# Scan and mixture of adapters on one core: stores of four chunks in 8 KB rows, other buffer counts, and orders as lists of names

## The chip, the core and the metric

The kernel runs on one core of one Trainium2 chip. Its engines are TensorE (PE in the profile), VectorE (DVE), ScalarE (ACT), GpSimd (POOL) and SyncE (SP), which here only issues DMAs. The metric is the device time of one execution in microseconds; the kernel before has a median of 202.84 us over 3 runs (202.61 to 203.44).

## What is computed

A linear recurrence over 6400 steps for 8 sequences of 128 channels, and then, on its 51200 output rows x, a mixture of adapters: of 8 experts of rank 16 the two with the highest logits are taken, weighted by a softmax over the two, and their outputs are added to x.

```python
for t in range(S):                       # a, b: [8, 6400, 128]
    h = a[:, t] * h + b[:, t]
    out[:, t] = h
x = out.reshape(51200, 128)
logits = x @ w_gate                      # [51200, 8]
# w: softmax over the two largest logits of each row, zero for the others
# out[row] = x[row] + sum over e of w[row, e] * ((x[row] @ A[e]) @ B[e])
```

With 8 x 16 = 128 the adapters of all experts are one 128x128 matrix A, whose product z is multiplied by the weights of the experts before the second matrix B. All inputs and the output are float32; 52.4 MB are read and 26.2 MB are written.

## The kernel before

The rows are cut into 100 chunks of 512 (names end in the chunk's number); a chunk is four blocks of 128 rows. What happens to a chunk falls into a front and a back.

**Front** (`load`, line 692; `front`, line 748). SP loads a and b of two chunks at a time, 512 KB each, into one of `NL` = 6 places of `a_tm` and `b_tm` (line 707). A partition takes eight rows in succession, 4 KB; the first four chunks are loaded singly, in 2 KB rows. The transposes `A`, `B` and `P` on PE (line 728) bring channels to the partitions in `pA` and `pB`, two places of PSUM each: `P93`, for example, transposes b of chunk 93 and a of chunk 94. ACT copies `pA` to `a_st` (`ae`, line 746), and DVE scans (`sc`, line 784) into `xT`, f16, which has `NX` = 24 places of one chunk.

**Logits and weights** (`zlogits`, line 795; `gating`, line 816). A unit is four or six blocks. PE multiplies each block of `xT` by A and the gate (`Z`, line 804), ACT copies the result to one of `NZ` = 120 places of `zl` (`ze`, line 810). For a group of one to four units DVE and POOL find the two largest logits, and ACT takes a sigmoid; the steps are `g1` to `g8`.

**Back** (`back_part`, line 899). POOL or DVE multiplies z by the weights (`mu`, `md`, lines 913 and 917), PE transposes the product (`T`, line 926), ACT or DVE copies it to `zwT` (`te`, lines 932 and 935), PE adds x and the product with B in `pO` (`D`, lines 940 and 941), and ACT or DVE copies the sum to `outt` (`oe`, `od`, lines 955 and 952), which has `NO` = 72 places of one block.

**Store** (`store`, line 976). SP stores two chunks at a time, 512 KB (line 986), the last four singly. A partition holds four rows in succession of each chunk, so a row of a store is 2 KB. `xblock` (line 665) picks the columns of `xT` that make a block: with four rows to a partition every fourth column belongs to one block, a step of 8 bytes.

```python
def xblock(b):
    return xcols(b // J).rearrange("d (p j) -> d j p", j=J)[:, b % J, :]
...
dst = out[r0 : r0 + m * C, :].rearrange("(h p j) d -> p h j d", p=128, j=J)
view = outt[:, q : q + m * J, :].rearrange("p (h j) d -> p h j d", j=J)
```

**Order.** Every step is an `Op` with the ops that it depends on. `schedule` (line 330) goes through the ops by a rank: a base by the chunk, and a number of `NUDGE` (line 30). With `WINDOW` at 0 the order on each engine is that of the ranks. Which engine takes a step is in `GATE_DVE`, `TE_ACT`, `MU_DVE` and `OE_DVE`. `waits` (line 400) gives each op the semaphores that it waits for. Each engine, and SP's queue of DMAs, works strictly in its order: what stands behind a waiting op waits too. A load waits until the transposes of the pair six places earlier are done, a scan until `D` of the chunk 24 earlier is done, a copy to `outt` until the store that held its places has landed.

Of the kernel before, what the change touches and what calls it, by code (L numbers as in the profile page):

```python
# [10 lines left out]
PERIOD = 6  # L11
FREE = {"pe": 0.0, "act": 0.105, "dve": 0.082, "pool": 0.044, "sp": 0.0}
SEEN = {"pe": 0.06, "act": 0.04, "dve": 0.055, "pool": 0.08, "sp": 0.0}
SELF = {"pe": 0.0, "act": 0.035, "dve": 0.035, "pool": 0.078, "sp": 0.0}
PE_WAIT = 0.08
PE_FREE = 0.1
SP_MARGIN = 2.0
LAND_MARGIN = 1.0
Q_RATE = {3: 4.2e-3, 5: 2.1e-3, 7: 2.1e-3}
SCAN_SELF = 0.13  # L20
ISSUE = {"sp": 0.52, "act": 0.45}
LOAD_RATE = 387e3
STORE_RATE = 413e3
DMA_START = 0.3
DMA_SEEN = 1.15
DMA_DEPTH = 9
FIRST_ISSUE = 0.7
FIRST_WORK = 0.73
TABLES = 1.32
NUDGE = {  # L30
# [182 lines left out]
}  # L213
WINDOW = {'pe': 0.0, 'act': 0.0, 'dve': 0.0, 'pool': 0.0, 'sp': 0.0}
START = (-999, "", 0)
FIRST = -9999
EARLY = -400
LEAD = [1, 2]
# [886 lines left out]
```

## Time and profile before

| | |
|---|---|
| time, median of 3 runs | 202.84 us |
| span of the profiled execution, first to last instruction | 200.9 us |
| bytes moved by DMA, mean rate | 79.26 MB, 395 GB/s |
| landing of a load of 512 KB, from its issue (median) | 13.3 us for a, 13.5 us for b |
| landing of a store of 512 KB (median) | 13.4 us |
| mean granted clock of TensorE | 0.997 |

The profiled execution is one run, and its span stands beside the median of the runs: the difference, 1.9 us, lies outside of the first and last instruction. In the profile a line such as L986 is a line of the kernel; `out<-in` names what an instruction writes and reads; SPq is SP's queue of DMAs; PEld are the weight loads of PE, which overlap its matmuls. The busy time of PE holds the pipeline's latency of each matmul, so starts that follow each other say more of PE than durations.

### The profile page before, as it was taken

The numbers are of one execution on the slowest core, as the hardware profiler recorded it, in microseconds if no ns is written. First come the engines' busy times: TensorE is split into PE (matmuls) and PEld (weight loads), VectorE is DVE, ScalarE is ACT, GpSimd is POOL, SyncE is SP. The second block draws the span as 40 slices with busy tenths as digits, with TensorE's granted clock in tenths as the row PEclk, the third lists the DMA queues.
The fourth block names the chain that finished last, engine by engine and source line by source line (L and its number), as shares of the span: only waits on it lengthen the run. The fifth ranks groups of instructions, "written<-read, shape, count | busy, mean of one in ns | idle before, by whom it ended". The sixth has DMA issues, their size and how long they took to land.

```text
span 200.9 us, 7611 instructions
## 1 busy us (share of the span) xinstructions
PE 177.7 (88%) x3192; PEld 155.9 (78%) x3192; DVE 176.2 (88%) x283; ACT 175.8 (88%) x327; POOL 136.9 (68%) x176
## 2 busy tenths in 40 slices
PE   6888978999899969999988999899999997898970
PEld 6766867888688858888878888787888886787860
DVE  1699999999999968999897999798899998999971
ACT  2589998999779969999997999899999998899970
POOL 1331559498989887797987797868876466767420
PEclk9999999999999999999999999999999999999998
DMA  6999999999999999999999999999999999999985
GB/s 216 378 412 408 411 405 401 411 406 404 414 409 400 412 416 409 401 417 407 409 413 409 410 409 412 413 410 411 417 408 410 414 410 409 406 381 387 357 338 215
DMA packets 29065, 79.26 MB, mean 395 GB/s; under 512 B 2664, under 2 KB 2920, under 8 KB 29032
## 3 DMA queue, kind: packets, MB, share of 16 engines
q1 hardware_dynamic: 28456, 78.39, 99.0%
q8 instruction: 25, 0.41, 0.8%
q10 hardware_dynamic: 576, 0.40, 0.7%
q14 instruction: 8, 0.07, 0.1%
HBM read 52.56 MB, written 26.21 MB: 392 GB/s over the span
## 4 chain that ended last, share of the span: by engine, by line
DMA 33%; PE 27%; DVE 16%; ACT 15%; SPq 5%; issue 2%; DVEq 0%; ACTq 0%
DMA a_tm<-in_a_dram 26%; DVE xT L784 9%; DMA out_dram<-outt 7%; ACT zl L810 5%; PE pZ L804 5%; SPq L707 5%; PE pB L728 5%; PE pA L728 5%; ACT outt L955 4%; PE pO L940 4%; PE pO L926 4%; ACT a_st L746 4%; PE pO L941 3%; DVE zwT L935 2%; ACT zwT L932 2%
## 5 line engine op out<-in xcount | busy, mean ns | idle before, releaser
L784 DVE TENSOR_TENSOR_SCAN xT<-a_st,xT,pB 128x512 f16<-128x512 f32 x96 | 120.4, 1254 | 7.1 <-PE pA L728 4.3
L913 POOL TENSOR_TENSOR zw<-zl,g 128x512 f16<-128x512 f32 x88 | 92.7, 1067 | 27.9 <-DVE g L880 19.6
L728 PE MATMUL pB<-ident_f,b_tm 64*128 64x64 f32 (+1 forms) x784 | 69.3, 229 | 6.8 <-DMA a_tm<-in_a_dram 6.7
L728 PE MATMUL pA<-ident_f,a_tm 64*128 64x64 f32 (+1 forms) x784 | 69.8, 230 | 0.5 <-DMA b_tm<-in_b_dram 0.3
L746 ACT COPY a_st<-pA 128x512 f32<-128x512 f32 x100 | 63.3, 638 | 4.1 <-PE pA L728 3.3
L728 PEld LDWEIGHTS pB<-ident_f,b_tm 64*128 64x128 f32 (+1 forms) x784 | 56.4, 139 | 11.8 <-DMA a_tm<-in_a_dram 8.3
L810 ACT COPY zl<-pZ 128x816 f32<-128x816 f32 (+1 forms) x69 | 59.7, 865 | 2.0 <-PE pZ L804 1.7
L728 PEld LDWEIGHTS pA<-ident_f,a_tm 64*128 64x128 f32 (+1 forms) x784 | 56.8, 139 | 5.6 <-issue 0.4
L955 ACT COPY outt<-pO 128x512 f32<-128x512 f32 x88 | 55.9, 640 | 3.9 <-PE pO L941 3.0
L940 PE MATMUL pO<-ident_h,xT 128*128 128x128 f16 x368 | 51.6, 222 | 1.3 <-ACT zwT L932 1.0
L941 PE MATMUL pO<-cst_h,zwT 128*128 128x128 f16 x368 | 50.5, 219 | 0.0
L940 PEld LDWEIGHTS pO<-ident_h,xT 128*128 128x128 f16 x368 | 40.2, 113 | 4.3 <-ACT zwT L932 1.4
L804 PE MATMUL pZ<-cst_h,xT 128*128 128x136 f16 x400 | 35.9, 225 | 4.9 <-DVE xT L784 2.0
L941 PEld LDWEIGHTS pO<-cst_h,zwT 128*128 128x128 f16 x368 | 36.8, 100 | 0.0
L926 PE MATMUL pO<-ident_h,zw 128*128 128x128 f16 x368 | 35.2, 220 | 1.4 <-ACT outt L955 1.1
L804 PEld LDWEIGHTS pZ<-cst_h,xT 128*128 128x128 f16 x400 | 26.3, 114 | 9.1 <-DVE xT L784 4.3
L926 PEld LDWEIGHTS pO<-ident_h,zw 128*128 128x128 f16 x368 | 22.9, 97 | 4.7 <-ACT outt L955 1.3
L935 DVE COPY zwT<-pO 128x512 f16<-128x512 f16 x57 | 22.9, 407 | 4.0 <-PE pO L926 3.7
L932 ACT COPY zwT<-pO 128x512 f16<-128x512 f16 x35 | 21.9, 630 | 4.7 <-PE pO L926 4.3
L850 POOL TENSOR_TENSOR L<-k,m 128x192 f32<-128x192 f32 (+2 forms) x16 | 8.4, 524 | 6.2 <-DVE m L848 6.1
L872 POOL TENSOR_TENSOR k<-k,L 128x192 f32<-128x192 f32 (+1 forms) x17 | 9.4, 556 | 4.3 <-DVE L L868 3.0
L846 POOL TENSOR_TENSOR L<-L,k 128x192 f32<-128x192 f32 (+1 forms) x15 | 8.6, 576 | 5.4 <-DVE L L843 4.7
(58 smaller groups left out, 112.2 us busy)
## 6 DMA issues: line engine op xcount, KB each, us to landing
a_tm<-in_a_dram SPq DMA_DIRECT2D x48, 512.0 KB, 13.3
b_tm<-in_b_dram SPq DMA_DIRECT2D x48, 512.0 KB, 13.5
out_dram<-outt SPq DMA_DIRECT2D x47, 512.0 KB, 13.4
a_tm<-in_a_dram SPq DMA_DIRECT2D x4, 256.0 KB, 4.3
out_dram<-outt SPq DMA_DIRECT2D x4, 256.0 KB, 3.6
b_tm<-in_b_dram SPq DMA_DIRECT2D x3, 256.0 KB, 5.1
out_dram<-outt SPq DMA_DIRECT2D x1, 496.0 KB
b_tm<-in_b_dram ACTq DMA_DIRECT2D x1, 256.0 KB, 3.4
```

Source lines behind the costliest of these rows:

```text
L728: last = eng["pe"].transpose(*args)
L746: lambda: eng["act"].copy(a_st[c % NA][:, :], pA[:, c % 2, :]), fr(c, "ae"))
L784: last = eng["dve"].tensor_tensor_scan(out=x[:, s0:s1], data0=a_st[c % NA][:, s0:s1], data1=pB[:, c % 2, s0:s1], initial=init, op0=ALU.mul ...
L804: last = eng["pe"].matmul(pZ[:, k // (n // 2), o : o + W], xblock(b0 + k), Awg_h)
L810: return eng["act"].copy(zl[:, zb : zb + n, :].rearrange("p (h k) w -> p h (k w)", h=2), pZ[:, :, 0 : n // 2 * W])
L913: lambda: eng["pool"].tensor_tensor(out=wv, in0=zv, in1=gv, op=ALU.mult), ba(gi, c, "mu"))
L926: last = eng["pe"].transpose(ptile[:, k * 128 : k * 128 + 128], zz[:, k, :], ident_h[:, :])
L932: lambda: eng["act"].copy(zt, ptile[:, 0 : n * 128]), ba(gi, c, "ta"))
L935: lambda: eng["dve"].tensor_copy(zt, ptile[:, 0 : n * 128]), ba(gi, c, "te"))
L940: eng["pe"].matmul(dst, xblock(b0 + k), ident_h[:, :], start=True, stop=False)
L941: last = eng["pe"].matmul(dst, zt[:, k * 128 : k * 128 + 128], B_h, start=False, stop=True)
L955: lambda: eng["act"].copy(ov, bv), ba(gi, c, "oe"))
```

## The change

Stores take four chunks (1 MB) but for the first two (two chunks each) and the last four (single ones, as before). Over the chunks of one store a partition holds all rows in succession: 16 rows or 8 KB for four chunks, 4 KB for two. So the columns of `xT` that make a block are now every sixteenth of four chunks, a step of 32 bytes. `xT` is one tile, and the logits of a unit wait for the scan of the last chunk of its store; a place of `xT` is free when `D` of all four chunks of the store that held it are done. The fronts run on to the end of the store's chunks before the logits.

`NX` goes from 24 to 32, `NO` from 72 to 80, `NZ` from 120 to 96. Ahead of `P6` to `P13` PE runs four transposes of the identity each (`fi7` to `fi14`, into `pA`), which wait for the copy that frees the place. The planner with its ranks is gone: the order of each engine and of SP's queue is a list of names, and the engine of a step follows from the list in which it stands. DVE has 68 copies to `zwT` (60 before), 3 to `outt` (7) and 9 products with the weights (12); the other 32, 97 and 91 are ACT's, ACT's and POOL's; of the gating steps that either DVE or POOL can take, DVE has 28 (20 before).

The diff, cut to its core:

```diff
-TAIL_UNITS = [4, 4, 4, 4]
-HEAD_UNITS = [4, 4, 4]
-FILL = {}
-NX = 24
-NZ = 120
-NO = 72
-STORE_TAIL = [1, 1, 1, 1]
+UNITS = [4] * 3 + [6] * 62 + [4] * 4
+GROUPS = [1, 2] + [4] * 15 + [2, 1, 1, 1, 1]
+STORES = [2, 2] + [4] * 23 + [1] * 4
+FILL = {k: 4 for k in range(7, 15)}
+NX = 32
+NZ = 96
+NO = 80
+ORDER = {
+    "pe": (
...
+    "sp": (
+        "la1 la0 lb1 la2 la3 lb3 lb2 la4 lb4 la6 lb6 la8 lb8 la10 lb10 la12 lb12 la14 lb14 la16 lb16 la18 lb18 la20 "
+        "lb20 lb24 la22 lb22 la24 la30 la26 lb26 la28 st0 lb32 lb28 lb30 la36 la32 st4 la34 lb34 lb36 lb38 st2 la38 "
+        "lb40 la40 st8 la42 st12 lb42 la50 la44 lb44 la46 lb46 la48 lb48 st16 lb50 la54 la52 lb52 st20 lb54 la56 lb56 "
...
+        "lb76 la76 st36 lb78 la78 la80 la82 lb80 st40 lb82 lb84 la84 st44 st48 la86 lb86 la88 lb88 la90 lb90 st52 "
+        "la92 lb92 lb94 la94 la96 st56 lb96 la98 st60 st64 lb98 st68 st72 st76 st80 st84 st88 st92 st97 st96 st98 "
+        "st99 "
+    ),
+}
...
+        self.order = {e: [named[name] for name in ORDER[e].split()] for e in self.ENGINES}
...
-            return xT[c % NX][:, :]
+            o = c % NX * C
+            return xT[:, o : o + C]
 
         def xblock(b):
-            return xcols(b // J).rearrange("d (p j) -> d j p", j=J)[:, b % J, :]
+            s0, n = tile_of[b // J]
+            o = s0 % NX * C
+            return xT[:, o : o + n * C].rearrange("d (p j) -> d j p", p=128)[:, b - s0 * J, :]
...
+        def filler(c):
+            def f(e):
+                for _ in range(FILL[c]):
+                    last = e.transpose(pA[:, c % 2, 0:128], ident_f[:, :], ident_f[:, :])
+                return last
+
+            if c in FILL:
+                o_fi[c] = P.add("pe", f"fi{c}", FILL[c], get(o_ae, c - 2) + [o_id], f)
...
         def zlogits(u):
             b0, n = units[u]
-            c1 = (b0 + n - 1) // J
+            c1 = sum(tile_of[(b0 + n - 1) // J]) - 1
...
-            xlast[ch % NX] = o_D[c]
+            s0, m = tile_of[c]
+            for k in range(s0, s0 + m):
+                if xlast.get(k % NX, (None, []))[0] != s0:
+                    xlast[k % NX] = (s0, [])
+                xlast[k % NX][1].append(o_D[c])
...
-            dst = out[r0 : r0 + m * C, :].rearrange("(h p j) d -> p h j d", p=128, j=J)
-            view = outt[:, q : q + m * J, :].rearrange("p (h j) d -> p h j d", j=J)
+            dst = out[c * C : (c + m) * C, :].rearrange("(p j) d -> p j d", p=128)
+            view = outt[:, q : q + m * J, :]
```

In SP's list `la` and `lb` are loads of a and b (of a pair from chunk 4 on), and `st` is a store, each with its first chunk. The end of the old list, in the same names, is `la92 lb92 st58 la94 lb94 la96 st60 lb96 la98 st62 lb98 st64 st66` and then the stores that are left.

More of the change, by code (lines that the diff above doesn't have):

```diff
@@ L853, in maxes @@
[L853 to L862 removed]
+                return P.add("dve" if kind == 8 else "pool dve", f"g{kind}_{gi}", nb, deps, f)
@@ L937, in delta, with tr @@
-            def delta():
-                for k in range(n):
+            def tr(e):
+                for k in range(J):
+                    last = e.transpose(ptile[:, k * 128 : k * 128 + 128], zz[:, k, :], ident_h[:, :])
+                return last
+            o_T[c] = P.add("pe", f"T{c}", J, [o_mu[c], o_ih] + free + (o_wu if c < 2 else []), tr)
+            o_te[c] = P.add("dve act", f"te{c}", J, [o_T[c]] + get(o_D, c - NW),
+                            lambda e: copy(e, zt, ptile[:, 0:C]))
@@ L956, in back_part @@
-            for k in range(n):
+                    e.matmul(dst, xblock(b0 + k), ident_h[:, :], start=True, stop=False)
+                    last = e.matmul(dst, zt[:, k * 128 : k * 128 + 128], B_h, start=False, stop=True)
+                return last
+            o_D[c] = P.add("pe", f"D{c}", J, [o_te[c]], delta)
+            s0, m = tile_of[c]
[3 more added lines that the diff above has]
+                xlast[k % NX][1].append(o_D[c])
@@ L1012, in load_next, with fronts @@
-        def load_next(c):
-            if c not in o_la:
-                load(c, 1 if c < HEAD else HC)
-        nf, nb = 0, 0
+        def fronts(c):
+            s0, n = tile_of[c]
+            return s0 + n
+        nf, nb, ns = 0, 0, 0
         for gi, (u0, n) in enumerate(groups):
@@ L1032, in bass_associative_scan_2x2__then__mixture_of_adapters_kernel @@
                 nb += 1
+                if sum(stores[ns]) == nb:
+                    store(*stores[ns])
+                    ns += 1
         P.schedule()
-        waits = P.waits(s_eng, s_dma)
+        waits = P.waits()
         def run(name, handle):
```

607 lines of the change are left out of this document (171 added, 436 removed), and 235 rows, old and new, of tables (NUDGE, ORDER).

## The prediction

> **What bounds the kernel now.** First the page: the busy shares, the slices of the DMA engines, and the queue that SP feeds.
>
> ```profile
> span 200.9 us, 7611 instructions
> PE 177.7 (88%) x3192; PEld 155.9 (78%) x3192; DVE 176.2 (88%) x283; ACT 175.8 (88%) x327; POOL 136.9 (68%) x176
> DMA  6999999999999999999999999999999999999985
> GB/s 216 378 412 408 411 405 401 411 406 404 414 409 400 412 416 409 401 417 407 409 413 409 410 409 412 413 410 411 417 408 410 414 410 409 406 381 387 357 338 215
> ...
> q1 hardware_dynamic: 28456, 78.39, 99.0%
> ...
> HBM read 52.56 MB, written 26.21 MB: 392 GB/s over the span
> ```
>
> No engine is full, and each of the four has 23 us or more idle. The 16 DMA engines have no idle slice before the last five: from 5 us to 175 us they move about 410 GB/s. Next, the DMA view of three stretches: 12 to 24 us (only loads, in 4 KB rows: the first store is issued at 24.97 us), 60 to 160 us (two loads to a store), and 178.5 to 184.5 us, behind the last load, which SP issues at 162.58 us and which lands some 14 us later. There only stores run, in 2 KB rows. Columns of the q1 lines: packets, MB, share of the 16 engines.
>
> ```profile
> q1 hardware_dynamic: 1346, 4.88, 102.0%
> ...
> q1 hardware_dynamic: 14522, 40.77, 102.5%
> ...
> q1 hardware_dynamic: 1207, 2.32, 101.6%
> ...
> 24.97 0.40 SPq L986 DMA_DIRECT2D out_dram<-outt  x1
> ...
> 162.58 1.77 SPq L707 DMA_DIRECT2D b_tm<-in_b_dram  x1
> ...
> DMA to landing us min/median/max: 4.1/13.5/15.7
> ```
>
> That is 4.88/12 = 407 GB/s for loads, 40.77/100 = 408 for the mix and 2.32/6 = 387 for stores alone, with the engines full each time. So up to the last load the kernel is bound by the DMA queue. It is not bound tightly, as the waits show (first for the whole run, then for 160 to 180 us; total, times, longest):
>
> ```profile
> PE pB L728 <- DMA a_tm<-in_a_dram: 6.7, 10, 2.0
> ...
> PE pB L728 <- DMA a_tm<-in_a_dram: 1.5, 3, 1.1
> ```
>
> PE stands 6.7 us before loads that haven't landed. A faster queue can give back about that much before the order of the engines' own work is the limit. Last, the tail: scans of chunks 93 and 99 and the last copy to outt on DVE, and the DMA by stretch.
>
> ```profile
> 168.49 1.28 DVE L784 TENSOR_TENSOR_SCAN xT<-a_st,xT,pB 128x512 f16<-128x512 f32 x1
> 181.55 1.27 DVE L784 TENSOR_TENSOR_SCAN xT<-a_st,xT,pB 128x512 f16<-128x512 f32 x1
> 195.91 0.69 DVE L952 COPY outt<-pA 128x512 f32<-128x512 f32 x1 [0.58 <-PE pA L941]
> ...
> core 0: us, PE busy (x) PEld busy (x) DVE busy (x) ACT busy (x) POOL busy (x), PEclk, DMA share, GB/s
> 185.00:190.00 5.00, 4.90 (x80) 4.29 (x79) 4.13 (x19) 4.45 (x10) 2.53 (x8) 1.00 0.92 355
> 190.00:195.00 5.00, 3.69 (x60) 3.18 (x58) 4.41 (x11) 3.91 (x9) 1.36 (x3) 1.00 0.91 340
> 195.00:198.00 3.00, 0.87 (x16) 0.69 (x13) 1.02 (x2) 0.74 (x2) 0.00 (x0) 1.00 0.75 289
> 198.00:200.90 2.90, 0.00 (x0) 0.00 (x0) 0.00 (x0) 0.00 (x0) 0.00 (x0) 0.78 0.46 177
> ```
>
> From the scan of chunk 93 to the last copy 28.1 us pass, with DVE seldom idle. The last store is issued right behind that copy and ends the span 4.3 us later. The DMA share drops from 1.02 to 0.92, 0.91 and 0.75, about 0.5 + 0.6 + 0.8 = 1.9 us of engine time unused. The end is set by the engines' last chunks, with the stores close behind.
>
> **The change, part by part.**
>
> *8 KB rows.* By the rates above a 4 KB row takes an engine 16 x 4096 B / 407 GB/s = 161.0 ns and a 2 KB row 16 x 2048 / 387 = 84.7 ns. Two small rows cost 8.3 ns more than one of twice the size. If that is a price per row, an 8 KB row takes 4 x 84.7 - 3 x 8.3 = 313.8 ns, 24.9 ns less than four of 2 KB. A store of four chunks is 512 such rows of 2 KB, 128 of 8 KB, eight to an engine: 0.20 us saved. 23 of these stores save 4.6 us, and the first two, in 4 KB rows, 0.1 us: at most 4.7. The lower end is 0, because the mix, where two thirds of the stores run, moves 408 GB/s with 2 KB rows in it, no less than the loads alone. The rows support both ends, so I take half: -2.4 us, of which -1.7 before the last load lands (16 of the 23 stores and the first two) and -0.7 behind it.
>
> [...]
>
> *Order of loads and stores.* In the old order the loads that chunk 94 needs stand behind the stores of 60 chunks; in the new, behind those of 56, but b of that pair stands ahead of a. Two 512 KB stores less and one load more, at 512 KB / 408 GB/s = 1.28 us each: 1.3 us earlier for the point at which the tail above starts. The last load stands behind 68 stored chunks, not 64, 2.6 us later; but its scan (181.55 us before, 33 DVE operations ahead of the end) now has only 23 operations behind it, which covers that. PE's 1.5 us of waits in that stretch say that -1.3 can be used, 0 if something else is late. I take -1.0.
>
> *The end.* The last four-chunk store (92 to 95) can't leave before its fourth copy, and holds the queue 2.6 us where a pair holds it 1.28: 0 to +1.3. On DVE 61 operations, not 53, follow the scan of chunk 93: four more copies of zwT, three fewer to outt, seven more small gating steps of about 0.2 us.
>
> ```profile
> L935 DVE COPY zwT<-pO 128x512 f16<-128x512 f16 x57 | 22.9, 407 | 4.0 <-PE pO L926 3.7
> L932 ACT COPY zwT<-pO 128x512 f16<-128x512 f16 x35 | 21.9, 630 | 4.7 <-PE pO L926 4.3
> L952 DVE COPY outt<-pO 128x512 f32<-128x512 f32 x4 | 2.7, 674 | 0.1
> L955 ACT COPY outt<-pO 128x512 f32<-128x512 f32 x88 | 55.9, 640 | 3.9 <-PE pO L941 3.0
> L913 POOL TENSOR_TENSOR zw<-zl,g 128x512 f16<-128x512 f32 x88 | 92.7, 1067 | 27.9 <-DVE g L880 19.6
> L917 DVE TENSOR_TENSOR zw<-zl,g 128x512 f16<-128x512 f32 x12 | 8.3, 695 | 0.0
> ```
>
> 4 x 0.41 - 3 x 0.67 + 7 x 0.2 = +1.0 us of DVE work, beside gaps in the tail. Together 0 to +2.3; I take +0.4. Over the whole run eight zwT copies go from ACT to DVE, four outt copies to ACT, three products to POOL: ACT -8 x 0.63 + 4 x 0.64 = -2.5 us, DVE +8 x 0.41 - 4 x 0.67 - 3 x 0.70 = -1.5 and eight gating steps, about +2, more. No total moves by more than 3 us: nothing, under the DMA queue.
>
> *Fillers.* Eight times four transposes of ident_f. The head's transposes of that shape start 0.44 us apart per four:
>
> ```profile
> 1.53 2.82 PE L611 MATMUL pO<-ident_f 128*128 128x128 f32 x12 [1.53 <-POOL ident_f L584]
> ...
> 5.46 0.60 PE L728 MATMUL pB<-ident_f,b_tm 128*128 128x128 f32 x4
> 5.90 0.60 PE L728 MATMUL pA<-ident_f,a_tm 128*128 128x128 f32 x4
> ...
> sum 18.00, PE 15.16 PEld 12.66 DVE 17.41 ACT 16.32 POOL 6.55; mean PE 2.53 PEld 2.11 DVE 2.90 ACT 2.72 POOL 1.09
> ```
>
> 8 x 0.44 = 3.5 us against 18.00 - 15.16 = 2.8 us of idle PE from 10 to 28 us. Some 0.7 us may push the fronts back; that stays hidden while loads are queued for up to twelve chunks. I take 0; without that cover it is +0.7.
>
> *Waiting for four scans.* The first logits of a group of four chunks wait for its last scan, up to three scans or 3.8 us longer. What hides it is the lead of the fronts, which is 16 to 18 chunks in the old order and about 20 in the new, out of 32 places of x (24 before). Output places are 20 chunks, at 1.9 us a chunk far over a store's landing; the 96 places of z hold 24 chunks where the order keeps some 13. All 0. If the lead is used up, PE stands up to 3.8 us at a group, which is part of the third rival's side.
>
> *x stepped by 32 bytes.* Blocks of x were read with a step of four fp16 and are now read with one of 16. The 800 weight loads of x (lines 804 and 940) show what the small step costs:
>
> ```profile
> L940 PEld LDWEIGHTS pO<-ident_h,xT 128*128 128x128 f16 x368 | 40.2, 113 | 4.3 <-ACT zwT L932 1.4
> L941 PEld LDWEIGHTS pO<-cst_h,zwT 128*128 128x128 f16 x368 | 36.8, 100 | 0.0
> ...
> 175.50 0.22 PE L940 MATMUL pO<-ident_h,xT 128*128 128x128 f16 x1
> ...
> 175.89 0.22 PE L941 MATMUL pO<-cst_h,zwT 128*128 128x128 f16 x1
> ```
>
> 13 ns longer than a load of dense columns, but the eight matmuls still start 0.39/7 = 56 ns apart: hidden. The lower end is 0; the upper is a doubled 56 ns at each, 800 x 0.056 = 45 us of PE. I take 0, as the row is at 0, and keep the other end as a rival.
>
> **Sum.** -2.4 - 1.0 + 0.4 = -3.0 us on the profiled span: 200.9 - 3.0 = 197.9. The median of the runs, 202.84, is 1.9 above the span, so the time is **199.8 us**.
>
> **Rivals.**
>
> *More is given back (chance 0.16).* The row price holds in full (-4.7) and the order's -1.3 too, with no cost at the end: -6.0, under the 6.7 us that PE waits. Time 196.8. For it: stores alone show the full 5% against loads. Against: the mix doesn't.
>
> *The rows do nothing (0.15).* The mix is at the rate of loads, so row size may not matter there, or rows are cut to 4 KB on the way. What is left is order and end, -1.0 + 0.4: 202.2.
>
> *x becomes slow to load (0.15): slower.* Place: lines 804 and 940. PE has 23.2 us idle, of which 1.5 lie ahead of the first transpose and 5.0 behind 195 us (3.00 - 0.87 and the 2.9 after), so about 16.7 can be used. It decides from 16.7/800 = 21 ns more between starts. At a doubled 56 ns it is 45 - 16.7 - 3.0 = +25: 228. Against it: a step of 32 bytes already occurs, in the writes of the fronts' transposes to pA and pB, and costs nothing:
>
> ```profile
> 176.66 0.22 PE L728 MATMUL pB<-ident_f,b_tm 64*128 64x64 f32 x1
> ...
> 177.03 0.22 PE L728 MATMUL pB<-ident_f,b_tm 64*128 64x64 f32 x1
> ```
>
> Six steps in 0.37 us, 62 ns to a pair of f32 transposes, next to the 56 ns of a dense f16 matmul. [...]
>
> *SP stands at a four-chunk store (0.10).* SP takes its queue in order. The store of chunks 4 to 7 stands ahead of the loads of pair 34, with loads for only eight chunks beyond the front issued; that of 12 to 15 with seven. These hold 8 x 0.5 MB / 408 GB/s = 10.3 us and 9.0 us. If the fourth chunk's products (1.07 us each on POOL) and copies come later, the DMA engines run dry for about two products' time at each of the two: +4.3 - 3.0 = +1.3, 204.1.
>
> **Numbers.** The forecast itself has 0.44; its own range is 198.0 to 201.8. About 0.5%, 1 us, is what a measurement here can tell. Faster: 0.44 + 0.16 and 0.04 of the rows that do nothing, 0.64. Same: 0.11 of these and 0.01 of the stall, 0.12. Slower: 0.15 and 0.09, 0.24. The range 196.2 to 204.6 holds the forecast, the first two rivals and most of the stall; it leaves out the slow loads of x and a little on either side, 0.2.
>
> **What would show it.** Rows: q1's packets fall from 28456 to about 19000 (9088 rows and 23 x 16 ends of transfers fewer), and stores alone run at some 410 to 418 GB/s. Order: PE's wait for a_tm falls below 6.7 us. x: the loads at the lines of 804 and 940 stay near 113 ns and the starts 56 ns apart. Queue: no slice of DMA under 9 between 5 and 175 us. The forecast is wrong if the mix stays at 408 GB/s, if PE's idle time vanishes, or if the tail from the scan of chunk 93 grows beyond 28 us by more than the loads come earlier.

## The result, and the profile after

The changed kernel takes 208.25 us (median of 4 runs, 207.29 to 208.93), the kernel before, on the same chip, 202.73 us: a ratio of 1.026, with an interval of 1.023 to 1.030. It is slower; the forecast was 199.8 us, in a range of 196.2 to 204.6. The profiled execution has a span of 206.1 us.

The page after, with the lines that answer to those of before:

```profile
span 206.1 us, 7671 instructions
...
PE 187.9 (91%) x3224; PEld 168.1 (82%) x3224; DVE 175.7 (85%) x292; ACT 176.5 (86%) x324; POOL 135.2 (66%) x171
...
DMA  6999999999999999999999999999999999986682
GB/s 218 380 414 409 410 402 408 375 395 417 412 410 420 405 402 408 413 413 410 413 414 403 421 403 416 408 417 424 410 408 417 414 418 424 376 291 261 280 353 94
...
q1 hardware_dynamic: 19000, 78.39, 95.0%
```

The packets are the 19000 that the forecast counted, and from 5 us to 175 us no slice of the DMA is under 9. Each slice is 5.15 us; the last six, from 175 us, hold the loss: the engines move 291, 261 and 280 GB/s in three of them, where before none of the last six but the very last was under 338. The reader sees two places more, slices 8 and 9 (36 to 46 us) at 375 and 395, to which the experiments come back.

The waits of PE over the whole run, then the longest wait of ACT after 160 us (total, times, longest):

```profile
PE pO L576 <- ACT outt L298: 2.0, 1, 2.0
...
PE pB L415 <- DMA a_tm<-in_a_dram: 0.6, 2, 0.4
PE pA L415 <- DMA a_tm<-in_a_dram: 0.6, 1, 0.6
...
ACT outt L298 <- DMA out_dram<-outt: 2.4, 2, 2.2
```

PE's wait for loads fell from 6.7 us to 1.2. New is a copy to outt that waits 2.2 us until a store has landed, with PE standing 2.0 us behind it. Of the stores, one is cut; its rows in the list of DMA issues, before and after:

```profile
out_dram<-outt SPq DMA_DIRECT2D x1, 496.0 KB
```

```profile
out_dram<-outt SPq DMA_DIRECT2D x1, 992.0 KB
```

That is `SPLIT = {68: [124, 4]}` (line 241 before, line 14 after), whose value the diff leaves as it is, and which neither the diff as printed above nor the prediction names. In `store` it cuts the store that begins at chunk 68 into one of 124 partitions and one of 4:

```python
cuts = SPLIT.get(c, [128])
...
    return [e.dma_start(dst[p : p + n], view[p : p + n]) for p, n in zip(lows, cuts)]
```

The store grew from two chunks to four, so its large piece from 496 KB to 992. The end after, by stretches (columns as in the prediction: engines, granted clock, DMA share, GB/s), and two single microseconds of it:

```profile
core 0: us, PE busy (x) PEld busy (x) DVE busy (x) ACT busy (x) POOL busy (x), PEclk, DMA share, GB/s
180.00:185.00 5.00, 4.95 (x78) 4.38 (x74) 4.82 (x16) 4.88 (x11) 2.34 (x4) 1.00 0.88 318
185.00:190.00 5.00, 3.04 (x48) 2.65 (x45) 3.61 (x11) 2.73 (x7) 2.92 (x5) 1.00 0.68 265
190.00:195.00 5.00, 4.86 (x53) 4.56 (x54) 3.17 (x18) 4.17 (x11) 2.11 (x3) 0.66 0.64 265
195.00:200.00 5.00, 2.97 (x40) 2.28 (x40) 2.50 (x9) 2.87 (x6) 0.00 (x0) 1.00 0.84 341
200.00:206.00 6.00, 0.00 (x0) 0.00 (x0) 0.00 (x0) 0.00 (x0) 0.00 (x0) 0.63 0.33 130
...
202.00:203.00 1.00, 0.00 (x0) 0.00 (x0) 0.00 (x0) 0.00 (x0) 0.00 (x0) 0.50 0.21 82
203.00:204.00 1.00, 0.00 (x0) 0.00 (x0) 0.00 (x0) 0.00 (x0) 0.00 (x0) 0.50 0.19 72
```

From 200 us on no engine but the DMA works, and from 202 us the DMA's share is 0.2, as if some 3 to 4 of the 16 DMA engines were left with work while the others had none. Before, the span ended 4.3 us after the last copy, with no such stretch. So the trace points to the cut store. ACT's wait lies at 186.2 to 188.4 us, in the second of these stretches, ahead of the copy of chunk 88; `outt` has places for 20 chunks, so these are the places of chunk 68. And a few engines that still carry the store's share seem to end the run. Whether that is so, the first experiment asks.

### The profile page after: what moved, and what is told of

It reads as the page before. It is cut to its first block, busy times and chain, and to the rows that moved or that the text cites. A ratio compares the mean times of both kernels' runs of the same rounds, so it can differ in the third digit from the quotient of the medians.

```text
span 206.1 us, 7671 instructions
## 1 busy us (share of the span) xinstructions
PE 187.9 (91%) x3224; PEld 168.1 (82%) x3224; DVE 175.7 (85%) x292; ACT 176.5 (86%) x324; POOL 135.2 (66%) x171
## 2 busy tenths in 40 slices
DMA packets 19609, 79.26 MB, mean 385 GB/s; under 512 B 2296, under 2 KB 2552, under 8 KB 16632
## 4 chain that ended last, share of the span: by engine, by line
PE 42%; DMA 22%; DVE 3%; ACT 2%; issue 2%; SPq 0%; ACTq 0%
DMA out_dram<-outt 13%; PE pB L415 12%; DMA a_tm<-in_a_dram 9%; PE pO L586 7%; PE pO L576 7%; PE pZ L498 6%; PE pO L587 5%; PE pA L415 3%; ACT outt L298 2%; DVE xT L480 1%; DVE zw L567 1%; PE pB L586 1%; PE pB L587 0%; DVE zwT L298 0%; PE pB L576 0%
## 5 line engine op out<-in xcount | busy, mean ns | idle before, releaser
L433 ACT COPY a_st<-pA 128x512 f32<-128x512 f32 x100 | 60.2, 622 | 7.6 <-PE pA L415 7.2
L298 ACT COPY outt<-pO 128x512 f32<-128x512 f32 x89 | 52.8, 613 | 4.3 <-PE pO L587 3.6
L586 PE MATMUL pO<-ident_h,xT 128*128 128x128 f16 x368 | 54.7, 234 | 0.4 <-issue 0.3
L586 PEld LDWEIGHTS pO<-ident_h,xT 128*128 128x128 f16 x368 | 46.5, 144 | 2.6 <-DVE zwT L298 0.4
L587 PEld LDWEIGHTS pO<-cst_h,zwT 128*128 128x128 f16 x368 | 39.8, 108 | 0.4 <-issue 0.4
L498 PEld LDWEIGHTS pZ<-cst_h,xT 128*128 128x128 f16 x400 | 30.8, 146 | 3.3 <-issue 1.4
L298 DVE COPY zwT<-pO 128x512 f16<-128x512 f16 x62 | 25.4, 413 | 2.7 <-PE pO L576 2.4
L298 ACT COPY zwT<-pO 128x512 f16<-128x512 f16 x30 | 18.4, 617 | 1.1 <-PE pO L576 0.7
L543 POOL TENSOR_TENSOR L<-L,k 128x192 f32<-128x192 f32 (+2 forms) x16 | 9.2, 575 | 5.8 <-DVE L L541 5.3
L480 DVE TENSOR_TENSOR_SCAN xT<-a_st,pB 128x512 f16<-128x512 f32 (+1 forms) x8 | 7.5, 938 | 5.5 <-PE pB L415 5.5
```

The lines of the kernel that those rows point to most:

```text
L298: return e.copy(dst, src) if e is eng["act"] else e.tensor_copy(dst, src)
L433: lambda e: e.copy(a_st[c % NA][:, :], pA[:, c % 2, :]))
L480: last = e.tensor_tensor_scan(out=x[:, s0:s1], data0=a_st[c % NA][:, s0:s1], data1=pB[:, c % 2, s0:s1], initial=init, op0=ALU.mult, op1=AL ...
L498: last = e.matmul(pZ[:, k // (n // 2), o : o + W], xblock(b0 + k), Awg_h)
L543: d3 = wide(5, [d3], lambda e: e.tensor_tensor(out=ll, in0=ll, in1=kk, op=ALU.add))
L586: e.matmul(dst, xblock(b0 + k), ident_h[:, :], start=True, stop=False)
```

## Experiments

Each time is beside runs of the kernel before on the same chip, whose medians were 202.62 to 202.70 us. Edits are against the changed kernel unless it is said otherwise. A time holds more than the span from the first to the last instruction: 1.8 to 1.9 us more in these runs of the kernel before and in its variants, but 2.0 to 3.7 us in runs of the changed kernel and its variants. Where small differences count, the spans of the runs are given too; the last section says what the traces show there.

### The cut taken away, in both kernels; another cut; the rows

`a_whole68`:

```diff
-SPLIT = {68: [124, 4]}
+SPLIT = {}
```

> The changed kernel, with the store of chunks 68 to 71 issued whole, not as 124 and 4 partitions. Split theory: the part of 124 partitions does not run on all 16 DMA engines, so a few of them have to move most of 1 MB while the others run ahead and then stand idle; that is why the DMA share falls to 0.88, 0.68 and 0.64 between 180 and 195 us, why ACT waits 2.2 us for a store to land, and why the stores behind land 22 us after their issue. Then this kernel has a DMA share near 1.0 up to about 190 us, no such wait, and a time of 200 to 203 us. Rival, slow loads of x (113 ns before, 145 after): the split hardly matters, the tail stays, 207 to 209 us.

Measured: 203.42 us (12 runs, 202.04 to 205.24), ratio 1.002 [0.999, 1.005]. The cut carries 4.8 us, nearly all of the slowdown, though the time is 0.4 us over the range expected; ACT's waits for a store fall from 2.4 us to 0.4. What is left is no gain, but two groups of times: six runs from 202.0 to 202.7, and six from 204.1 to 205.2. The median lies between them. The groups are there in the spans too: 200.0 to 200.6 and 201.2 to 202.0 us.

`b_whole68`, the same edit in the kernel before.

> The kernel before, with its store of chunks 68 and 69 issued whole, not as 124 and 4 partitions. Split theory: here the split part is 496 KB, half as much, and the tail has a DMA share of 0.92, 0.91 and 0.75 from 185 to 198 us; issued whole it gains 0.5 to 1.5 us, 201.3 to 202.3 us. If the split is harmless: 202.8 within 0.3.

Measured: 203.51 us (12 runs, 203.19 to 203.77), ratio 1.004 [1.003, 1.005]. The expectation missed, with its sign: in the kernel before the same cut, at half the size, brings 0.9 us.

`a_split64`: `SPLIT = {68: [64, 64]}`.

> The changed kernel, with the store of chunks 68 to 71 issued as 64 and 64 partitions. If what costs is that 124 partitions run on few engines, two parts of 64 cost nothing and the time is that of the store issued whole, within 0.5 us. If it is one more transfer and one more place in SP's queue, the time stays near 208 us.

Measured: 203.29 us (202.25 to 205.02), ratio 1.004 [1.001, 1.007]. A cut into two halves does nothing either way, so it is not the cutting that costs.

`a_2k_whole68`, without the cut and with the old access inside the new stores:

```diff
-            s0, n = tile_of[b // J]
-            o = s0 % NX * C
-            return xT[:, o : o + n * C].rearrange("d (p j) -> d j p", p=128)[:, b - s0 * J, :]
+            return xcols(b // J).rearrange("d (p j) -> d j p", j=J)[:, b % J, :]
...
-            dst = out[c * C : (c + m) * C, :].rearrange("(p j) d -> p j d", p=128)
-            view = outt[:, q : q + m * J, :]
+            dst = out[c * C : (c + m) * C, :].rearrange("(h p j) d -> p h j d", p=128, j=J)
+            view = outt[:, q : q + m * J, :].rearrange("p (h j) d -> p h j d", j=J)
```

> The changed kernel with the store of 68 to 71 whole, and with the layout of before inside each store of four chunks: rows of 2 KB, x stepped by 8 bytes; order, buffers and fillers stay. It isolates rows and step. Prediction's term: the 8 KB rows save 0 to 4.7 us, so this one is slower than its pair with 8 KB rows by up to 4.7 us, 2.4 taken. Slow loads of x: those loads go from 145 back to 113 ns, PE gets some 5 us shorter (8 ns at 400 places of line 586, 4 ns at 400 of line 498), and this kernel is as fast or faster by up to 3 us.

Measured: 204.93 us (203.93 to 205.65), ratio 1.010 [1.006, 1.013]: against `a_whole68` the 8 KB rows bring 1.5 us, though the two groups blur it.

### How many engines a store has

`a_120_8`: `SPLIT = {68: [120, 8]}`.

> The changed kernel with its one cut store (chunks 68 to 71) cut into 120 and 8 partitions in place of 124 and 4; all else is as in the changed kernel. Theory: the store of 124 partitions ran on 4 of the 16 DMA engines alone (the trace after 202 us shows a DMA share of 0.19 to 0.21 while only stores are left), because of its number of partitions and not because it is cut. [...] So here the time comes back to that of the uncut store, 202.5 to 204.0 us, and the last stretch of the trace has no microseconds at a share near 0.2. Rival 1, any store that isn't of all 128 partitions runs on few engines: 207 to 209 us. Rival 2, a second lane of small transfers costs by its own existence: 205 to 207 us.

Measured: 204.23 us (4 runs, 203.98 to 204.96), ratio 1.009 [1.006, 1.011]. The last microsecond of its trace in which the DMA share is over 0.05:

```profile
198.00:199.00 1.00, 0.00 (x0) 0.00 (x0) 0.00 (x0) 0.00 (x0) 0.00 (x0) 1.00 0.54 213
```

The next one has 0.04, so no stretch near 0.2 is left, and 4.0 us of the 4.8 are back with a cut as uneven as the first: it is the number 124 that costs. A share of 0.2 is 3.2 of 16 engines. The packets of q1 say more, here with the store whole (`a_whole68`), at 120 and 8, and at 64 and 64 (`a_split64`):

```profile
q1 hardware_dynamic: 19008, 78.39, 97.0%
```

```profile
q1 hardware_dynamic: 19015, 78.39, 97.2%
```

```profile
q1 hardware_dynamic: 19024, 78.39, 97.0%
```

With 124 and 4 there are 19000. The rows are the same each time, and the differences are packets under 512 B: by the pages 2304 with the store whole, 2320 at 64 and 64 and 2296 at 124 and 4, so that the 7 packets more of 120 and 8 make 2311. The prediction counted 16 such packets to a transfer. The kernel before, with 156 transfers on q1, and the changed one, with 133, agree, with 2664 - 2296 = 368 = 23 x 16 of them:

```profile
DMA packets 29065, 79.26 MB, mean 395 GB/s; under 512 B 2664, under 2 KB 2920, under 8 KB 29032
```

```profile
DMA packets 19609, 79.26 MB, mean 385 GB/s; under 512 B 2296, under 2 KB 2552, under 8 KB 16632
```

So where the whole store has 16, the two pieces of 120 and 8 have 23, those of 64 and 64 have 32, and those of 124 and 4 have 8. That the large piece of 124 and 4 ran on four engines is an estimate of mine, from these 8 packets for two pieces and the share of about 0.2 at the end; no view shows the engines one by one, and no run shows how the number of partitions sets the number of engines. The time lies a little over the range expected. Three of the four runs have spans of 202.0 to 202.9 us, at or over the upper group of `a_whole68`, and one of 200.4; with four runs it can't be told whether the cut itself costs the rest.

### Where the two groups come from

Three edits of the uncut kernel, each for a suspect of mine. `a_first_single` stores the first four chunks singly (`STORES` begins with `[1, 1, 1, 1]`), because the DMA of `a_whole68` dips between 35 and 45 us, where the first store runs. `a_end_pairs` stores chunks 84 to 95 in pairs. `a_no_fill` has `FILL = {}`.

> The changed kernel without the cut at chunk 68 (203.42 us), with the first four chunks stored singly in 2 KB rows in place of two pairs in 4 KB rows. Theory: the dip of the DMA to 332 to 363 GB/s between 37 and 47 us, which the kernel with 2 KB rows and the kernel before do not have, comes with the first store in 4 KB rows, whose single packets took up to 0.5 to 0.9 us; it costs (412-350)/412 of some 7 us, about 1 us. Then the dip is gone and the time is 202.2 to 202.8 us. Rival: the dip comes from the first stores meeting the loads whatever their rows are, or what is lost there is caught up by the waits of the end; then 203.0 to 203.8 us.

> The changed kernel without the cut at chunk 68 (203.42 us), with chunks 84 to 95 stored in pairs (512 KB, 4 KB rows) in place of three stores of four chunks. Theory: at 180 to 190 us the DMA falls to 330 to 345 GB/s because a store of 1 MB waits for its fourth chunk while the first three lie ready; in pairs the DMA is fed earlier, and (412-340)/412 of 10 us, up to 1.7 us, comes back in part: 202.0 to 202.9 us, with the DMA share of 180 to 190 us above 0.95. Rival: the end is set by the copies to outt (the last of them ends at 197.2 us in the uncut kernel, 4.3 us before the last landing), and earlier stores only leave the queue empty later: 203.2 to 203.8 us, last copy at 197 us again.

> The changed kernel without the cut at chunk 68 (203.42 us) and without the fillers on TensorE in the first fronts. Theory of the prediction: the fillers fill time in which TensorE has nothing to do and cost and bring nothing: 203.2 to 203.6 us, scans of the first chunks at the same times to within 0.3 us. Rival 1, they raise the granted clock early and so bring something: 203.8 to 204.8 us without them, with the granted clock below 1 in the first 30 us. Rival 2, they hold up the transposes of the first loads (scan of chunk 4 ends 1.3 to 3 us later than in the kernel before): 202.4 to 203.0 us without them, scan 4 at 13 us.

Measured: 204.12 us (6 runs, 203.79 to 204.93; ratio 1.008 [1.006, 1.010]), 203.72 us (12 runs; 1.003 [1.000, 1.006]) and 203.77 us (12 runs; 1.002 [0.999, 1.005]). The first two theories missed, and the third, that the fillers do nothing, misses its range by 0.2 us: with single first stores the dip is still there (346 and 324 GB/s in the two stretches from 35 us), and the other two have both groups again, 202.1 to 203.0 and 204.4 to 205.6 with pairs at the end, 201.8 to 203.4 and 204.1 to 205.7 without the fillers. The fillers cost and bring nothing that these runs tell. But now there were traces of both kinds, and they differ from the first transposes on. Time line of PE in the trace of `a_whole68` with the dip (its span of 202.0 us is one of the upper group; start, time, and in brackets what it waited for):

```profile
1.53 2.82 PE L319 MATMUL pO<-ident_f 128*128 128x128 f32 x12 [1.53 <-POOL ident_f L303]
5.00 1.12 PE L415 MATMUL pA<-ident_f,a_tm 128*128 128x128 f32 x4 [0.65 <-DMA a_tm<-in_a_dram]
...
6.76 1.06 PE L415 MATMUL pB<-ident_f,b_tm 128*128 128x128 f32 x4
7.62 1.06 PE L415 MATMUL pA<-ident_f,a_tm 128*128 128x128 f32 x4
8.47 1.06 PE L415 MATMUL pB<-ident_f,b_tm 128*128 128x128 f32 x4
```

Four transposes take 1.06 us here until 9.3 us, and the eight behind them 1.81 us, where `a_head_order` below takes 1.12; the head of the kernel before, quoted in the prediction, has 0.60 for the same work. PE stood still for 0.65 us first: SP issues a of chunk 1 ahead of a of chunk 0 in the new list (`la1 la0`), and ACT's queue the B matrices ahead of b of chunk 0, so the first load that PE needs comes later. The first scan starts at 7.94 us, not 6.2.

`a_head_order` undoes that alone:

```diff
-        "la1 la0 lb1 la2 ...
+        "la0 la1 lb1 la2 ...
...
-        "cb lb0 ca cw ae0 ...
+        "lb0 cb ca cw ae0 ...
```

> The changed kernel without the cut at chunk 68, with the first loads issued in the former order: a of chunk 0 ahead of a of chunk 1 on SP, b of chunk 0 ahead of the B matrices on ACT's queue. The uncut kernel has two groups of times, 202.0 to 202.7 and 204.1 to 205.2 us. In its trace TensorE stands still for 0.65 us after the first twelve warming transposes (4.35 to 5.00 us), because a of chunk 0 is issued second; four transposes then take 1.06 us until 9.3 us, where they take 0.60 us later and in the traces with an early first scan, and the first scan begins at 7.9 us in place of 6.6. Theory: the gap restarts the time that TensorE needs until it runs fast, by luck of the moment; with the former order the gap is gone (first transposes of a at 4.1 to 4.3 us), the first scan begins at 6.2 to 7.1 us and the upper group of times disappears: median 202.0 to 202.6 us, all under 203.2. Rival, the two groups have another cause (the meeting of the first store with the loads at 37 to 47 us): two groups again, median 202.2 to 204.2 us.

`a_long_warm` keeps the new order of loads and fills the gap: the warming transposes `wu12` to `wu15` go ahead of `A0`.

> The changed kernel without the cut at chunk 68, with its loads in the new order and the second four warming transposes of TensorE moved ahead of the first transposes of a, so that the gap of 0.46 to 0.91 us is filled (four of them take 0.85 us at the slow rate); nothing else. If the gap itself is what makes TensorE stay slow, the upper group of times goes as with the former order of loads: first scan at 6.4 to 7.4 us, median 202.1 to 202.8 us, all under 203.4. If the late first load alone costs the time, both groups stay, median 202.2 to 204.2 us.

Measured: 202.41 us (12 runs, 201.65 to 203.75; ratio 0.999 [0.998, 1.001]) and 202.55 us (12 runs, 202.01 to 203.38; 0.999 [0.998, 1.001]). The group at 204 to 205 is gone in both, and in the second no load comes sooner: it is the gap that costs, not the late load. The spans say it more sharply: all twelve of `a_head_order` are 199.6 to 200.3 us, and eleven of `a_long_warm` 199.8 to 200.2, with one of 201.3. (Three runs in each lie at 203.2 to 203.8, over the upper end expected for `a_head_order`; but for that one they have 2.9 us or more outside of the span.) `a_head_order` in its trace:

```profile
4.14 1.06 PE L415 MATMUL pA<-ident_f,a_tm 128*128 128x128 f32 x4
...
5.85 1.06 PE L415 MATMUL pB<-ident_f,b_tm 128*128 128x128 f32 x4
6.70 0.83 PE L415 MATMUL pA<-ident_f,a_tm 128*128 128x128 f32 x4
7.37 0.60 PE L415 MATMUL pB<-ident_f,b_tm 128*128 128x128 f32 x4
```

PE is fast from 7.2 us. The starts show it, 0.85 us apart for each four transposes and then 0.44, as in the kernel before. The moment of change lay at 4.9 to 7.3 us without a gap and at 5.2 to past 10 with one. `a_120_8`, with a gap of 0.91 us, is fast from 5.3 us, so a gap need not bring a late start. What sets the moment, and whether the gap restarts anything, as the expectation took it, is not shown by any run. What the late start does later is seen from 35 to 45 us, first `a_whole68`, then `a_head_order`:

```profile
35.00:40.00 5.00, 5.00 (x98) 4.38 (x96) 4.82 (x5) 5.00 (x10) 4.81 (x6) 1.00 0.98 358
40.00:45.00 5.00, 5.00 (x104) 4.55 (x102) 4.65 (x7) 5.00 (x10) 4.45 (x6) 1.00 1.01 320
```

```profile
35.00:40.00 5.00, 5.00 (x96) 4.37 (x92) 4.82 (x7) 5.00 (x11) 4.77 (x7) 1.00 1.03 409
40.00:45.00 5.00, 4.95 (x102) 4.61 (x100) 4.74 (x8) 5.00 (x11) 3.02 (x5) 1.00 1.02 406
```

PE has next to no idle time there, so what it lost in the head it can't catch up, and its places of a_tm come free later. SP waits for them with its next loads, from 28 to 48 us for 13.6 us in `a_whole68` and 7.1 in `a_head_order`, and the DMA moves less: (409 - 358 + 406 - 320)/410 of 5 us, 1.7 us. The DMA engines are not idle, as the shares of 0.98 and 1.01 show: from 40 to 45 us a packet of q1 takes 183 ns on average (432 packets at 98.7% of 16 engines), where it takes 146 in `a_head_order` (555 at 101.4%). Why packets take longer there is not shown.

The traces of the changed kernel with 8 KB rows, the main one and eleven of its variants, bear the chain out. Where the first scan starts by 7.02 us (seven traces), the DMA moves 395 to 411 GB/s from 40 to 45 us; where it starts at 7.23 and 7.57, 362 and 357; at 7.92 to 8.09, 320 to 342.

`b_new_head` is the kernel before with the new order of the first loads.

```diff
+        sp, act = self.order["sp"], self.order["act"]
+        sp[0], sp[1] = sp[1], sp[0]
+        act.insert(0, act.pop(3))
```

> The kernel before with the changed order of the first loads alone: a of chunk 1 ahead of a of chunk 0, the B matrices ahead of b of chunk 0; the end and all else as before. Theory: TensorE then stands still for 0.4 to 0.9 us before its first transposes, and part of the runs starts slow: times in two groups, one near 202.7 and one 1.0 to 2.0 us above it, median 202.7 to 204.2 us, highest over 203.9. Rival, the kernel before has the slack to take it (its DMA never dips at 35 to 50 us, also where its first scan begins at 7.0 us): 202.4 to 203.2 us, no second group.

Measured: 202.61 us (11 runs, 202.21 to 202.90), ratio 1.000 [0.999, 1.001]; my theory missed. PE is slow until about 9 us in its trace, and its first scan starts at 8.0 us, but the scan of chunk 50 at 91.0, 0.3 us later than before. So the old order can take the late start, and the new one can't.

`a_head_pairs` joins `a_head_order` and `a_end_pairs`.

> The uncut kernel with both the former order of the first loads and the last stores of four chunks as pairs (a_head_order and a_end_pairs together). Theory: the upper group of times goes, and the lower group of a_end_pairs (202.1 to 202.45 us) is left: median 201.6 to 202.3 us, ratio to the kernel before 0.995 to 0.999. If the end is set by the copies and not by the stores, no better than a_head_order: 202.0 to 202.6 us. If the upper group has another cause: median 202.2 to 204.5 us.

Measured: 202.48 us (202.09 to 203.26), ratio 0.999 [0.998, 1.001]: no better than `a_head_order`. That the end waits for stores of four chunks costs nothing that can be measured.

### Size of the cut, and price of the rows again

`a_cut_small` is `a_head_order` with the cut at its old size (and `st70` behind `st68` in SP's list):

```diff
-STORES = [2, 2] + [4] * 23 + [1] * 4
-SPLIT = {}
+STORES = [2, 2] + [4] * 16 + [2, 2] + [4] * 6 + [1] * 4
+SPLIT = {68: [124, 4]}
```

> a_head_order with chunks 68 to 71 stored as two stores of two chunks, the first of them cut into 124 and 4 partitions as in the kernel before (496 KB on few engines, 4 KB rows). If the size decides: the four engines lag 496/4 - 496/16 = 93 KB behind the others, at some 26 GB/s for one engine (413/16) 3.6 us, which the idle DMA of the end takes up (shares 0.83, 0.67, 0.91, 0.68 in the four stretches of 5 us from 180 in a_head_order, 4.5 us in sum): 201.5 to 202.8 us, no last microseconds at a share near 0.2, perhaps the 0.8 us that the cut gained in the kernel before. If any cut of this kind is dear in the new order: 204 to 208 us.

Measured: 201.31 us (6 runs, 200.87 to 202.23), ratio 0.994 [0.992, 0.996]. It is faster than both kernels, 0.6% under the kernel before, and its spans are 198.8 to 200.0 us. To see whether the cut or the two smaller stores bring it, `a_pair_uncut` takes the cut away again (`SPLIT = {}`):

> a_cut_small (201.31 us) with the store of chunk 68 whole again, all else as there. If the cut brings the gain, as it brings 0.8 us in the kernel before, the time is that of a_head_order or a little less: 201.9 to 202.6 us. If the two stores of two chunks bring it: 201.0 to 201.6 us.

Measured: 202.42 us (12 runs, 201.85 to 203.78), ratio 1.000 [0.998, 1.003]. The spans are 199.8 to 200.6 us. The cut of 496 KB brings 1.1 us, much as the 0.9 us in the kernel before.

`b_two_cuts`, in the kernel before, cuts two stores of two chunks:

```diff
-SPLIT = {68: [124, 4]}
+SPLIT = {68: [124, 4], 70: [124, 4]}
```

> The kernel before with the stores of chunks 68 and 70 both cut into 124 and 4 partitions, 992 KB on few engines in place of 496. If the size decides: the four engines lag 186 KB, 7.2 us at 26 GB/s, less the idle DMA of the end of some 2.3 us (shares 0.92, 0.91, 0.72 in the three stretches from 185): 204.5 to 208 us, with last microseconds at a share of 0.2 to 0.25. If the cost belongs to the new order or to the 8 KB rows: 202.0 to 203.2 us.

Measured: 206.77 us (206.66 to 206.79), ratio 1.020 [1.019, 1.021], with old rows, old order and old buffers. Its end has the same look, and the DMA is short already at 175 us, where before it moved 381 GB/s:

```profile
175.00:180.00 5.00, 4.77 (x87) 4.29 (x87) 4.56 (x9) 4.88 (x11) 3.02 (x5) 1.00 0.71 265
...
200.00:205.00 5.00, 0.00 (x0) 0.00 (x0) 0.00 (x0) 0.00 (x0) 0.00 (x0) 0.63 0.25 98
```

Against the kernel before, with its one cut, that is 4.1 us more, and against the same kernel with no cut (203.51 us) 3.3. So the size decides, in either kernel: 992 KB on four engines (the estimate above) are 186 KB for each of them over an even share, 7.2 us by the estimate in the expectation, of which the idle DMA of the end hides a part.

`a_2k_head` is `a_head_order` with the edit of `a_2k_whole68`.

> a_head_order (202.41 us) with the rows of 2 KB inside its stores and the step of 8 bytes in xT; orders, buffers and places as they are. The forecast's first term says that the 8 KB rows bring 2.4 us (bounds 0 to 4.7), the first measurement 1.5 us. If they are worth what the forecast took: 204.5 to 205.2 us. If most of the 1.5 us was the upper group of times: 202.4 to 203.2 us. Between, 203.5 to 204.3 us: worth 1.1 to 1.9 us, and less than forecast.

Measured: 204.26 us (203.27 to 204.72), ratio 1.007 [1.005, 1.009]. Without the upper group the rows of 8 KB, with the step in xT that they ask for, are worth 204.26 - 202.41 = 1.85 us. Of that 1.3 us lie in the spans, whose medians are 201.35 us (201.2 to 202.1) and 200.05 (199.6 to 200.3); the rest lies outside of them. What the rows bring isn't seen as a faster mix. Stretch from 60 to 160 us of the kernel before, of `a_2k_head` and of `a_head_order`:

```profile
60.00:160.00 100.00, 93.84 (x1778) 83.20 (x1779) 90.93 (x129) 95.19 (x179) 79.42 (x94) 1.00 1.03 410
```

```profile
60.00:160.00 100.00, 94.21 (x1771) 83.30 (x1771) 92.62 (x141) 93.53 (x171) 78.71 (x94) 1.00 1.03 410
```

```profile
60.00:160.00 100.00, 97.39 (x1801) 88.60 (x1798) 94.22 (x143) 95.04 (x174) 79.76 (x95) 1.00 1.02 412
```

With the small rows PE is 94% busy at 410 GB/s; with the large ones it is 97% busy at 412. PE's waits for loads of a say the same: 3.0 us in all in `a_2k_head` and none in `a_head_order`, but PE is busy 3.6 us longer there. What the DMA gave, PE has taken up. The chain that ended last, as shares of the span by engine, of the kernel before and of `a_head_order`:

```profile
DMA 33%; PE 27%; DVE 16%; ACT 15%; SPq 5%; issue 2%; DVEq 0%; ACTq 0%
```

```profile
PE 74%; DVE 11%; ACT 9%; issue 4%; POOL 0%; POOLq 0%; DVEq 0%
```

In this trace of the changed kernel without its cut, and with the former first loads, the chain no longer runs over the DMA: PE sets the pace. (`a_pair_uncut`, which differs by one store, still has 17% of DMA in its chain.)

## Why the prediction was wrong

**Sum and result.** The medians make a ladder from the forecast to the result: 199.8 forecast; 201.31 with the order of the first loads and the size of the cut as before (+1.5); 202.42 without the gain of the small cut (+1.1; `a_head_order`, with a store of four chunks there, is the same, 202.41); 203.42 with the new order of the first loads (+1.0); 208.25 with the cut at its new size (+4.8). The medians of the spans make the same ladder: 197.9 forecast, then 199.1, 200.15, 200.9 and 206.25. The step of 1.0 us hangs on how many runs fall into the upper group. The forecast took 1.9 us outside of the span, as in the kernel before; in the changed one and its variants it was 2.0 to 3.7.

**The step that failed.** "A store of four chunks is 512 such rows of 2 KB, 128 of 8 KB, eight to an engine", and then all 23 stores alike. For the one at chunk 68 it is, by the estimate of four engines, 31 rows of its large piece to each of four and none to the other twelve. It stands in a line whose value the diff doesn't change, but it is used in a function that the diff does change, and its size is that of the store. The prediction priced a larger store at the queue's mean rate and never asked on how many engines it lies. No rival held it either; "SP stands at a four-chunk store" expected a dry queue early in the run, where the trace shows SP waiting for PE with its loads, and it said nothing of the end.

**Rows, -2.4.** The price of a row is right in kind, and the whole too large: 1.85 us by `a_2k_head`, 1.3 of them in the span. Stores alone run faster, as said (the queue's packets, MB and share of 16 engines from 191 to 195 us in `a_head_order`):

```profile
q1 hardware_dynamic: 214, 1.61, 97.7%
```

1.61/4 is 402 GB/s at a share of 0.977, or 420 at the 1.02 of full engines, where the forecast had 410 to 418. The mix, 60 to 160 us in the changed kernel:

```profile
q1 hardware_dynamic: 9507, 40.91, 101.0%
```

That is 409 GB/s, next to 408 before, at a share of 101.0% and not 102.5: the engines have a little less to do for the same bytes, and nothing makes use of it. The rows reach the engines whole, not in 4 KB pieces as a rival allowed: of the 19609 packets of the changed kernel 16632 are under 8 KB, and the other 2977 hold the 23 x 128 = 2944 rows. The prediction named a mix that stays as a sign that it is wrong: 1.7 of its 2.4 us were to come ahead of the last load. None did. The scan of chunk 93 in `b_whole68`, `a_2k_head` and `a_head_order`, three kernels without a cut:

```profile
168.33 1.28 DVE L784 TENSOR_TENSOR_SCAN xT<-a_st,xT,pB 128x512 f16<-128x512 f32 x1
```

```profile
166.97 1.28 DVE L478 TENSOR_TENSOR_SCAN xT<-a_st,xT,pB 128x512 f16<-128x512 f32 x1
```

```profile
167.06 1.28 DVE L480 TENSOR_TENSOR_SCAN xT<-a_st,xT,pB 128x512 f16<-128x512 f32 x1
```

The last two differ by the rows and the step alone, and reach this point at the same time, within 0.1 us. From there to the end of the span (201.7, 201.4 and 200.2 us) it is 33.37, 34.43 and 33.14 us: the rows bring 1.3 us behind this point, where -0.7 was forecast, and nothing ahead of it, where -1.7 was.

**x stepped by 32 bytes, 0.** This is probably where that part went. The loads of x after, and two matmuls of the same kind, seven starts apart:

```profile
L586 PEld LDWEIGHTS pO<-ident_h,xT 128*128 128x128 f16 x368 | 46.5, 144 | 2.6 <-DVE zwT L298 0.4
...
L498 PEld LDWEIGHTS pZ<-cst_h,xT 128*128 128x128 f16 x400 | 30.8, 146 | 3.3 <-issue 1.4
...
185.42 0.23 PE L586 MATMUL pA<-ident_h,xT 128*128 128x128 f16 x1
...
185.85 0.22 PE L587 MATMUL pA<-cst_h,zwT 128*128 128x128 f16 x1
```

A load takes 144 to 146 ns, where it took 113 to 114 ns, and these starts lie 0.43/7 = 61 ns apart, not 56. Over the run PE is busy for 186.4 us in `a_head_order` and 182.8 in `a_2k_head`: 3.6 us. The rival named the place and the point from which it decides, 21 ns a start, and 5 ns is far below that. But with the waits for loads of a down from 6.7 us to 1.2, PE had little cover left, and the smaller price seems to count: what left PE as waits, 3.0 us, came back as 3.6 us of busy time. The doubled start that the rival took, 56 ns more, is shown by no run: the start of a matmul moved by 5 ns. No run has 8 KB rows and the old step together, so what the step alone costs was not measured.

**Order, -1.0.** Right at its end: with 2 KB rows in both and no cut, the scan of chunk 93 starts at 166.97 us in the new order (`a_2k_head`, with the new buffers too) and at 168.33 in the old one (`b_whole68`), 1.4 us earlier, next to the 1.3 of the count. Not seen was the other end of the same list, the first loads, which cost 1.0 us by the slow start of PE; the part on the order looked at the last loads only.

**The end, +0.4.** It was placed low. Between the same two kernels the stretch from the scan of chunk 93 to the end of the span grows from 33.37 to 34.43 us: +1.1, inside the 0 to +2.3 of its bounds. In the changed kernel itself the cut store hides this. Scan of chunk 93 and the last copies to outt:

```profile
167.17 2.65 DVE L480 TENSOR_TENSOR_SCAN xT<-a_st,xT,pB 128x512 f16<-128x512 f32 x2
...
197.84 1.17 ACT L298 COPY outt<-pB 128x512 f32<-128x512 f32 x2 [0.54 <-PE pB L587]
```

31.8 us lie between them, against 28.1 before, and 7.1 us more to the end of the span, against 4.3.

So in three traces without a cut the change is worth -1.4 (order), +0.1 and -1.3 (rows, ahead of this point and behind it) and +1.1 (end), -1.5 us in all, where the forecast had -3.0. The other differences nearly cancel; what is missing is what the rows were to bring ahead of the last load.

**Fillers and waiting for four scans, 0.** `a_no_fill` shows no cost and no gain of the fillers beside the spread of its runs; waiting for four scans was not tested by itself.

## What to carry to other kernels

Before a transfer is made larger, look up every place that cuts or shapes it, also those that the change doesn't touch, and ask of each piece on how many DMA engines it lies; a piece on four engines is priced by its bytes over four engines and the slack at the end (here 992 KB cost 4.8 us in one kernel and 3.3 us in the other). When one bound is relaxed, price the small costs on the next engine as if it were full, because it is about to be. And when the first instructions are put in another order, check that the first matmuls still follow each other without a gap.

## What the runs showed of the hardware

- The granted clock says nothing of the slow start. Of `a_whole68`, the stretch in which four transposes take 1.06 us in place of 0.60, with the clock at 1.00:

```profile
5.00:7.00 2.00, 2.00 (x10) 2.00 (x11) 0.00 (x0) 0.59 (x1) 0.86 (x1) 1.00 1.06 309
```

- A gap of 0.4 to 0.9 us ahead of the first transposes can move the time at which PE runs fast from 4.9 to 7.3 us to past 10. In the changed kernel half of the runs with such a gap (`a_whole68`) have a span that is 1 to 2 us longer; the kernel before takes a slow start without loss (`b_new_head`).
- A cut that puts 496 KB on four engines, an estimate, makes the kernel before 0.9 us faster and the changed one, with the former first loads, 1.1 us. With 992 KB there it costs, against no cut, 4.8 us in the changed kernel and 3.3 us in the kernel before. Why the small one brings a gain is not settled.
- Part of what lies outside of the span goes with one packet. In eight traces of the changed kernel's variants a packet of 16 KB on q8, of the kind "instruction", runs after the last instruction. It ends 1.9 to 3.9 us behind the span, and 2.1 to 3.7 us of the run's time lie outside; in the traces of the changed kernel and its variants without it 2.0 to 2.3. Of `a_head_order`, from the end of its span at 200.2 us to 204.2:

```profile
q8 instruction: 1, 0.02, 2.1%
```

That run took 203.64 us, and another one of the same kernel with the same span 202.22. No experiment moved the packet, so that it costs this time is read from the traces and not shown.
